# Dispatch sums in two parts, in two PSUM banks, around the second head's maxima

## The chip, the cores and the metric

The kernel runs on one core of a Trainium2 chip. The metric is the device time of one execution in microseconds (us), as a median of several executions. Times inside an execution come from one profiled execution, counted from the start of its span.

## The reference

Causal attention over 8 batches of 12 heads (448 tokens, 64 wide) gives `x`, 3584 tokens by 768. A soft mixture of experts follows, with 8 experts of 4 slots each, 32 slots in all:

```python
logits = x @ phi                              # 3584 x 32
d = exp(logits - logits.max(0)); d /= d.sum(0) + 1e-09    # over the tokens
slot_input = d.T @ x                          # 32 x 768: the dispatch
h = maximum(slot_input[e] @ w1[e], 0); slot_out[e] = h @ w2[e]
c = exp(logits - logits.max(1)); c /= c.sum(1) + 1e-09    # over the slots
out = c @ slot_out
```

All inputs are float32.

## The kernel before

**Stages.** Attention runs over 48 pairs of heads, six pairs to a batch. `block(p)` works on pair `p` (heads `a = 2p` and `a + 1`) while it prepares heads `a + 2` and `a + 3`; 47 blocks (p = 0 to 46) and a shorter last one take the first three quarters of the time. The experts and the output follow, with the expert weights streaming in. No scheduler moves anything: every engine runs its instructions in the order in which the code is written, and the framework adds the waits between engines from the tiles that the instructions read and write.

**A block on TensorE.** `scores2(a)` finishes the scores of head `a` by adding its row maxima (the four matmuls `s<-r,k`); `scores1_all(a + 2)` starts the scores of head `a + 2`, and its first matmul puts the mask into the second bank of its tile (`s<-tri,identb`); then the same two steps for heads `a + 1` and `a + 3`. `attv_pair` multiplies the weights of both heads by the values (`po<-va,pt`). At the end of the block come the small pieces for the experts, then the transpose of the second head's maxima (`max_row(a + 3, 0)`, shown as `s<-ident,r`) and four transposes of attention outputs (`xm<-ident,x`). The next block begins again with `scores2`.

**Three score tiles.** `s_[0]` to `s_[2]` are PSUM tiles of 128 x 1024 float32, two banks of 512 columns each, used in turn. At the end of block `p` the tile `m = s_[(a + 1) % 3]` is free, and it serves as scratch: the pieces for the experts are written to it, and the transposed maxima to its last 128 columns. In the next block `scores1_all` fills the same tile with the scores of a new head.

**The way of the maxima.** VectorE finds the maxima of head `a + 3` (`max_keys`), TensorE transposes them into `m`, VectorE reduces them to one row (`max_row(a + 3, 1)`, shown as `mr<-s`), GpSimd spreads that row (`r<-mr`), and the next block's second `scores2` reads it.

**The pieces for the experts.** A batch's slot logits are summed over its six pairs in `lt` (`logits_t`). Its dispatch `d.T @ x` is computed in the blocks of the following batch: `dispatch_a` multiplies on TensorE (`s<-x,gs`, in four column groups, one for each 128 tokens; a float32 matmul stands as two records in the profile), and `dispatch_b` is one VectorE instruction, `si = al * si + m` (`SCALAR_TENSOR_TENSOR si<-si,al,s`), which adds the product to the running sum. What a block does depends on `p % 6`:

- `p % 6 = 3` (p = 9 to 45, seven blocks): two matmul groups for the logits, 128 columns of dispatch, then `mr`, `lt`, `si`. Block 3 has the logits alone.
- `p % 6 = 4` (p = 10 to 40, six blocks): 256 columns of dispatch in the second bank, then `mr`, `si`.
- `p % 6 = 0` (p = 12 to 42, six blocks): 384 columns of dispatch in the first bank, then `mr`, `si`.
- `p % 6 = 1` and `5` have logits alone, `2` has neither.

VectorE goes on with `norm(p, 2)` (`x<-po,sm`) at the head of the next block.

Of the kernel before, what the change touches and what calls it, by code (L numbers as in the profile page):

```python
# [17 lines left out]
P = 128  # L18
# [64 lines left out]
def attention_soft_moe(ctx: ExitStack, tc: tile.TileContext, qk, va, phi, w, out):  # L83
# [52 lines left out]
    def loads_v(p, eng=nc.sync):  # L136
        if p < NPAIR:
            eng.dma_start(out=va_[p % 2], in_=va[p])
# [30 lines left out]
    def load_w(n):  # L169
        if n < len(order):  # L170
            t = wtiles[order[n]] = slot(n, f"w{n}")
            q, g, c = place(n), (n + 2) // 4, WN * ((n + 2) % 4)
            if n < RES or n == NBUF or q >= RES + LATE2:
                nc.sync.dma_start(out=t, in_=w[g, :, c:c + WN])
            elif 4 <= q < RES and n > NBUF:
                if q % 4 == 3:
                    nc.sync.dma_start(out=group(n), in_=w[g])
            elif n % 2:
                t = group(n)
                nc.sync.dma_start(out=t[:, 2 * WN:] if q < RES else t, in_=w[g, :, c - WN:c + WN])  # L180
# [39 lines left out]
    def misc(name):  # L220
        return ps_1.tile([P, 512], F32, tag="m", name=name)
# [88 lines left out]
    def max_row(i, k, w=RW - RF, to=None):  # L310
        if i >= NHD:
            return
        if k == 0:
            st["rt", i] = misc(f"rt{i}") if to is None else to
            if w == AW:
                nc.tensor.matmul(st["rt", i][0:w, 0:P], r_[i % 2][:, RF:RF + w], ident, start=True, stop=True)
            else:
                nc.tensor.transpose(out=st["rt", i][0:w, 0:P], in_=r_[i % 2][:, RF:RF + w], identity=ident)
        else:
            mr = st["mr", i] = wk.tile([NQB, 32], F32, tag="mr", name=f"mr{i}", bufs=2)  # L320
            nc.vector.tensor_reduce(out=mr, in_=st.pop(("rt", i))[0:NQB, 0:P].rearrange("p (g t)->p t g", g=4),
                                    axis=AX.X, op=ALU.max, negate=True)
# [12 lines left out]
    def scores2(i, cs):  # L335
        if i >= NHD:
            return
        p, h = divmod(i, 2)
        s = st["s", i]
        k2 = k2_  # L340
        for c in cs:
            o, w, m = KS * h + P * c, S - CQ0[c], min(P, KS - P * c)
            nc.tensor.matmul(s[0:m, SCOL[c]:SCOL[c] + w], k2[:, o:o + m],
                             r2[:, h, CQ0[c]:S], start=False, stop=True, skip_group_check=True)
# [60 lines left out]
    def norm(p, k):  # L405
        if k == 0:
            sm = st["sm", p] = moe.tile([P, NQ], F32, tag="sm", name=f"sm{p}", bufs=2)
            nc.vector.tensor_scalar(out=sm, in0=po2[:, :, HD], scalar1=EPS, scalar2=None, op0=ALU.add)
        elif k == 1:
            nc.vector.reciprocal(out=st["sm", p], in_=st["sm", p])  # L410
        else:
            x, sm = x_of(p), st.pop(("sm", p))
            m = NCH - 1
            nc.vector.tensor_tensor(out=x[:, 0:m].rearrange("p c (h d)->p h c d", h=2),
                                    in0=po2[:, 0:2 * m, 0:HD].rearrange("p (h c) d->p h c d", h=2),
                                    in1=sm[:, 0:2 * m].rearrange("p (h c)->p h c", h=2).unsqueeze(3)
                                    .to_broadcast([P, 2, m, HD]), op=ALU.mult)
            for h in range(2):
                a = AW * h
                nc.vector.tensor_scalar(out=x[0:AW, m, HD * h:HD * h + HD], in0=po2[a:a + AW, 2 * m, 0:HD],  # L420
                                        scalar1=sm[a:a + AW, 2 * m:2 * m + 1], scalar2=None, op0=ALU.mult)
# [22 lines left out]
    def logits_t(j, g):  # L444

        nc.vector.tensor_tensor(out=lt, in0=g, in1=lt if j else mk, op=ALU.add)
# [31 lines left out]
    def dispatch_a(b, hf, sp, sl=slice(0, 384)):  # L478
        dn = st["dn", b]
        x, n = st["xn", 2 * b + hf], sl.stop - sl.start  # L480
        for c in range(NCH):

            nc.tensor.matmul(sp[32 * c:32 * c + 32, 0:n], dn[:, c], x[:, c, sl],
                             start=True, stop=True, skip_group_check=True)

    def dispatch_b(b, hf, sp, sl=slice(0, 384)):
        s = si[:, 384 * hf + sl.start:384 * hf + sl.stop]
        nc.vector.scalar_tensor_tensor(out=s, in0=s, scalar=st["al", b][:, 0:1], in1=sp[:, 0:sl.stop - sl.start],
                                       op0=ALU.mult, op1=ALU.add)
# [74 lines left out]
    def block(p):  # L564
        a, b = 2 * p, p // 6 - 1
        m6 = p % 6
        if p + 1 < NPAIR:
            loads_v(p + 1, nc.sync if p + 1 < NPAIR - 1 else nc.scalar)
        if p % 2 and p < 44 or p in (16, 30):
            load_w(st["w"])  # L570
            st["w"] += 1

        if p:
            norm(p - 1, 2)
        scores2(a, range(NCH))
        exps(a)
        if p == 0:
            copy_k2(0, h1)
            cast_q(1, h1)
            warm(START[3], pob)  # L580
            max_row(1, 0)
            max_row(1, 1)
            max_spread(1)
            sub_k(1, h1, nc.vector)
        elif p > 1:
            xcopy(p - 2)
            if p == NPAIR - 2:
                sub_q(p + 1, h0)
        scores1_all(a + 2)
        if p == 0:  # L590
            warm(START[2], pob)
        for k in range(3):
            max_keys(a + 2, k)
        if p == 0:
            cast_k(2, h0)
        scores2(a + 1, range(NCH))
        exps(a + 1)
        if p == 0:
            cast_k(2, h1)
        scores1_all(a + 3)  # L600
        if m6 == 2 and p > 6:
            logits_b(b)
        max_keys(a + 3, 0)
        late_k = p == 1
        if p == 1:
            sub_q(2, h0)
            sub_k(3, h0)
            sub_q(2, h1)
            load_qk(4, 0)
        elif p:  # L610
            sub_k(p + 2, h0 if late_k else slice(0, 2))
            if not late_k:
                load_qk(p + 4, 1)
            sub_q(p + 1, h1 if p == NPAIR - 2 else slice(0, 2))
            load_qk(p + 3, 0)
        else:
            sub_q(1, h0)
            sub_q(1, h1)
            load_qk(3, 0)
            sub_k(2, h0)  # L620
        copy_k2(p + 1)
        if m6 == 2 and p > 6:
            logits_d(b, lt)
        if p:
            cast_k(p + 3)
            cast_q(p + 2)
        else:
            cast_q(2)
            cast_k(3)
        if m6 == 3 and p > 6:  # L630
            logits_al(b)
        elif m6 == 4 and p > 6:
            logits_n(b)
        attv_pair(p)
        max_row(a + 2, 1)
        max_spread(a + 2)
        if p == 0:
            sub_k(2, h1)
            load_qk(4, 1)
        for k in (1, 2):  # L640
            max_keys(a + 3, k)
        for k in range(2):
            norm(p, k)

        m = s_[(a + 1) % 3]
        parts = []
        if m6 in (1, 3, 5) and p > 1:
            j = (m6 + 3) % 6
            logits_a(b if m6 == 1 else p // 6, (j, j + 1), m[:, 0:P])
        elif m6 == 2 and p > 6:  # L650
            logits_e(b, m, 0)
        if m6 == 3 and p > 6:
            parts = [(b, 0, slice(0, P), 512)]
        elif m6 == 4 and p > 6 and p < NPAIR - 2:
            parts = [(b, 0, slice(P, 3 * P), 512)]
        elif m6 == 0 and p > 6:
            parts = [(b - 1, 1, slice(0, 3 * P), 0)]
        for d, hf, sl, o in parts:
            dispatch_a(d, hf, m[:, o:o + sl.stop - sl.start], sl)
        max_row(a + 3, 0, to=m[:, 1024 - P:1024])  # L660
        max_row(a + 3, 1)
        if m6 == 2 and p > 6:
            logits_e(b, m, 1)
        max_spread(a + 3)
        if late_k:
            sub_k(p + 2, h1)
            load_qk(p + 4, 1)
        if m6 in (1, 3, 5) and p > 1:
            logits_t(j, m[:, 0:P])
        for d, hf, sl, o in parts:  # L670
            dispatch_b(d, hf, m[:, o:o + sl.stop - sl.start], sl)
        if p:
            xtrans(p - 1)

    for p in range(NPAIR - 1):
        block(p)
# [5 lines left out]
    i, b, p = NHD - 1, NB - 1, NPAIR - 1  # L682
# [70 lines left out]
    parts = [(hf, slice(a, a + 192)) for hf in range(2) for a in (0, 192)]  # L753
# [255 lines left out]
```

## Time and profile before

| | |
|---|---|
| median of 3 runs | 396.43 us (396.28 to 396.48) |
| the profiled execution | 396.08 us, of which the span of its instructions is 394.4 us |
| blocks and last block | to about 300 us |
| TensorE matmuls busy | 366.3 us, 93% of the span |
| VectorE, ScalarE, GpSimd busy | 295.2, 282.9 and 256.5 us |
| DMA | 119.17 MB, 302 GB/s over the span |

PE is TensorE's matmuls, PEld its weight loads, DVE VectorE, ACT ScalarE, POOL GpSimd. In a row of the timeline stand the start in us, the duration in us (of all instructions of a merged row together), the engine, the code line, the operation with the tile written, an arrow and the tiles read, the shapes and the count; in brackets the idle time of the engine before it, and what ended that. Nearly every row names line 67, the helper through which each instruction passes, so rows are told apart by their tiles.

### The profile page before, as it was taken

The numbers are of one execution on the slowest core, as the hardware profiler recorded it, in microseconds if no ns is written. First come the engines' busy times: TensorE is split into PE (matmuls) and PEld (weight loads), VectorE is DVE, ScalarE is ACT, GpSimd is POOL, SyncE is SP. The second block draws the span as 40 slices with busy tenths as digits, with TensorE's granted clock in tenths as the row PEclk, the third lists the DMA queues.
The fourth block names the chain that finished last, engine by engine and source line by source line (L and its number), as shares of the span: only waits on it lengthen the run. The fifth ranks groups of instructions, "written<-read, shape, count | busy, mean of one in ns | idle before, by whom it ended". The sixth has DMA issues, their size and how long they took to land.

```text
span 394.4 us, 13997 instructions
## 1 busy us (share of the span) xinstructions
PE 366.3 (93%) x5763; PEld 293.9 (75%) x5763; DVE 295.2 (75%) x835; ACT 282.9 (72%) x397; POOL 256.5 (65%) x215
## 2 busy tenths in 40 slices
PE   7899999999999999999999999999999989988940
PEld 3689889888988998898889888988986544533420
DVE  7887889888888888898888988888886675342550
ACT  5888899898898898888988988888864012431440
POOL 5998899898898888898988988889860000000000
PEclk9999999999999999999999999999999999998985
DMA  7868877788898788777997877887579999999996
GB/s 250 277 229 281 288 288 237 251 273 274 274 318 272 244 270 300 257 246 248 307 323 256 286 240 249 275 287 250 183 246 399 422 431 428 429 421 419 433 429 295
DMA packets 28720, 119.17 MB, mean 302 GB/s; under 512 B 3440, under 2 KB 3952, under 8 KB 26480
## 3 DMA queue, kind: packets, MB, share of 16 engines
q1 hardware_dynamic: 28512, 118.01, 83.2%
q8 instruction: 45, 0.74, 0.7%
q10 hardware_dynamic: 144, 0.27, 0.2%
q14 instruction: 19, 0.16, 0.1%
HBM read 107.25 MB, written 11.01 MB: 300 GB/s over the span
## 4 chain that ended last, share of the span: by engine, by line
PE 67%; DMA 9%; POOL 9%; DVE 5%; ACT 4%; issue 2%; SPq 0%; POOLq 0%; DVEq 0%; ACTq 0%
PE s L67 34%; PE po L67 20%; DMA w<-in_w_dram 8%; POOL r L67 6%; PE xm L67 4%; POOL ks L67 3%; PE so L67 2%; PE e L67 2%; PE pp L67 2%; PE rt L67 2%; DMA kraw<-in_qk_dram 1%; ACT qd L67 1%; DVE lm L67 1%; DVE lg L67 1%; ACT w L67 1%
## 5 line engine op out<-in xcount | busy, mean ns | idle before, releaser
L67 DVE TRANSPOSE_TENSOR_REDUCE r<-s 128x32 f32<-128x1024 f32 x96 | 119.5, 1245 | 7.7 <-PE s L67 4.9
L67 ACT ACTIVATE pt<-s 128x1024 f32<-128x1024 f32 x96 | 98.8, 1029 | 31.0 <-PE s L67 24.0
L67 PEld LDWEIGHTS po<-va,pt 128*64 128x64 f32 x3008 | 102.3, 138 | 11.8 <-issue 11.3
L67 PE MATMUL po<-va,pt 128*64 128x65 f32 x3008 | 109.2, 224 | 0.0
L67 POOL TENSOR_TENSOR r<-qraw,qd 64x896 fp32r<-64x896 f32 (+1 forms) x50 | 99.4, 1989 | 1.9 <-ACT qd L67 1.8
L67 POOL TENSOR_TENSOR ks<-kraw,ks 64x896 fp32r<-64x896 f32 (+1 forms) x48 | 89.7, 1870 | 4.1 <-ACT ks L67 0.5
L67 POOL TENSOR_SCALAR_AFFINE_SELECT r<-mr 14x448 fp32r<-14x448 f32 x96 | 61.6, 643 | 32.9 <-DVE mr L67 28.6
L67 PE MATMUL s<-qd,ks 128*66 128x64 f32 (+3 forms) x384 | 80.6, 321 | 0.0
L67 PE MATMUL s<-r,k 128*128 128x448 f32 (+3 forms) x384 | 65.2, 291 | 2.7 <-POOL r L67 2.7
L67 PEld LDWEIGHTS s<-r,k 128*128 128x128 f32 (+1 forms) x384 | 59.3, 176 | 8.6 <-POOL r L67 5.9
L67 PEld LDWEIGHTS s<-qd,ks 128*128 128x128 f32 (+1 forms) x384 | 52.5, 183 | 2.1 <-issue 0.9
L67 ACT ACTIVATE ks<-kraw 128x896 fp32r<-128x896 f32 (+1 forms) x49 | 45.0, 920 | 5.6 <-DMA kraw<-in_qk_dram 4.4
L67 ACT ACTIVATE k<-ks 64x896 fp32r<-64x896 f32 (+1 forms) x49 | 45.8, 936 | 1.2
L67 ACT ACTIVATE qd<-qraw 128x896 fp32r<-128x896 f32 (+1 forms) x48 | 44.6, 929 | 0.9 <-POOL r L67 0.7
L67 PE MATMUL s<-tri,identb 128*128 128x192 bf16 x192 | 39.6, 270 | 0.6
L67 DVE TENSOR_REDUCE r<-r 128x16 f32<-128x32 f32 x192 | 33.7, 176 | 5.0
L67 DVE TENSOR_REDUCE mr<-s 14x32 f32<-14x128 f32 x47 | 13.1, 279 | 21.4 <-ACT qd L67 14.8
L67 PE MATMUL xm<-ident,x 128*128 128x128 f32 x188 | 28.3, 273 | 0.0
L67 ACT ACTIVATE xts<-xm 128x512 f32<-128x512 f32 x46 | 27.2, 591 | 0.4 <-PE xm L67 0.4
L67 DVE TENSOR_SCALAR x<-po,sm 64x64 f32<-64x64 f32 x94 | 25.9, 276 | 0.7
L67 DVE COPY w<-pp 128x384 f32<-128x384 f32 x28 | 14.5, 553 | 15.4 <-PE pp L67 15.3
L67 DVE TENSOR_TENSOR x<-po,sm 128x384 f32<-128x384 f32 x47 | 25.2, 537 | 0.0
(151 smaller groups left out, 397.9 us busy)
## 6 DMA issues: line engine op xcount, KB each, us to landing
w<-in_w_dram SPq DMA_DIRECT2D x34, 768.0 KB, 6.7
kraw<-in_qk_dram SPq DMA_DIRECT2D x46, 448.0 KB, 4.4
qraw<-in_qk_dram SPq DMA_DIRECT2D x46, 448.0 KB, 4.5
w<-in_w_dram SPq DMA_DIRECT2D x5, 3072.0 KB, 25.0
va<-in_va_dram SPq DMA_DIRECT2D x47, 260.0 KB, 4.8
out_dram<-w SPq DMA_DIRECT2D x7, 1536.0 KB, 12.6
w<-in_w_dram SPq DMA_DIRECT2D x5, 1536.0 KB, 11.2
qk<-in_qk_dram SPq DMA_DIRECT2D x2, 448.0 KB, 7.1
```

Of the source, the lines that this page charges most:

```text
L67: return self._tc.keep_in_program_order(op(*args, **kwargs))
```

## The change

The two large dispatches are cut in two. The first part goes to the first bank of `m`, and its sum stands directly behind its matmuls in the code, ahead of the second part's matmuls and of the maxima; the second part goes to the second bank and its sum stays where the sum was. Where `p % 6 = 4` the parts are 128 and 128 columns wide, where `p % 6 = 0` they are 192 and 192. Where `p % 6 = 3` the dispatch stays whole, and the addition of the logits moves ahead of the maxima.

```diff
         elif m6 == 4 and p > 6 and p < NPAIR - 2:
-            parts = [(b, 0, slice(P, 3 * P), 512)]
+            parts = [(b, 0, slice(P, 2 * P), 0), (b, 0, slice(2 * P, 3 * P), 512)]
         elif m6 == 0 and p > 6:
-            parts = [(b - 1, 1, slice(0, 3 * P), 0)]
+            parts = [(b - 1, 1, slice(0, 192), 0), (b - 1, 1, slice(192, 384), 512)]
         for d, hf, sl, o in parts:
             dispatch_a(d, hf, m[:, o:o + sl.stop - sl.start], sl)
+            if o == 0:
+                dispatch_b(d, hf, m[:, 0:sl.stop - sl.start], sl)
+        if m6 == 3 and p > 1:
+            logits_t(j, m[:, 0:P])
         max_row(a + 3, 0, to=m[:, 1024 - P:1024])
         max_row(a + 3, 1)
...
-        if m6 in (1, 3, 5) and p > 1:
+        if m6 in (1, 5) and p > 1:
             logits_t(j, m[:, 0:P])
         for d, hf, sl, o in parts:
-            dispatch_b(d, hf, m[:, o:o + sl.stop - sl.start], sl)
+            if o:
+                dispatch_b(d, hf, m[:, o:o + sl.stop - sl.start], sl)
```

What stands on TensorE at the end of block 12 (`p % 6 = 0`), before; `s_80` is `m`, `r_91` the maxima of head `a + 3`, and the word in brackets names the semaphores that an instruction waits for:

```order
L67 MATMUL s_80<-x_97,gs 32x384 x4
L67 MATMUL s_80<-ident,r_91 76x128 [waits DVE_49]
L67 MATMUL xm_1463<-ident,x_99 128x128 [waits PE_49]
L67 MATMUL xm_1463<-ident,x_99 128x128 x3
L67 MATMUL s_81<-r_93,k_92 128x448 [waits Activation_49,Pool_49]
L67 MATMUL s_81<-r_93,k_92 128x320
L67 MATMUL s_81<-r_93,k_92 128x192
L67 MATMUL s_81<-r_93,k_92 66x64
L67 LDWEIGHTS identb
L67 MATMUL s_80<-tri_117,identb 128x192 [waits DVE_49]
```

and now:

```order
L67 MATMUL s_80<-x_97,gs 32x192 x4
L67 MATMUL s_80<-x_97,gs 32x192 [waits DVE_49]
L67 MATMUL s_80<-x_97,gs 32x192 x3
L67 MATMUL s_80<-ident,r_91 76x128
L67 MATMUL xm_1473<-ident,x_99 128x128 [waits PE_49]
L67 MATMUL xm_1473<-ident,x_99 128x128 x3
```

The wait for VectorE has moved from the transpose to the first matmul of the second part, ahead of it in TensorE's queue.

VectorE at the same place, before (`po` is what `attv_pair` wrote):

```order
L67 TENSOR_SCALAR sm_1451<-po 128x7 [waits PE_49]
L67 RECIPROCAL sm_1451<-sm_1451 128x7 [waits DVE_49]
L67 TENSOR_REDUCE mr_1459<-s_80 14x32 [waits PE_49,Activation_49,Pool_49]
L67 SCALAR_TENSOR_TENSOR si<-si,al_1109,s_80 128x384
L67 TENSOR_TENSOR x_97<-po,sm_1451 128x2x3x64 [waits DVE_49]
```

and now:

```order
L67 TENSOR_SCALAR sm_1456<-po 128x7 [waits PE_49]
L67 RECIPROCAL sm_1456<-sm_1456 128x7 [waits DVE_49]
L67 SCALAR_TENSOR_TENSOR si<-si,al_1109,s_80 128x192 [waits PE_49,Activation_49]
L67 TENSOR_REDUCE mr_1469<-s_80 14x32 [waits PE_49,Pool_49]
L67 SCALAR_TENSOR_TENSOR si<-si,al_1109,s_80 128x192
L67 TENSOR_TENSOR x_97<-po,sm_1456 128x2x3x64 [waits DVE_49]
```

The first sum stands ahead of `mr` with a wait of its own for TensorE, and the second is half as wide as the sum was.

VectorE at the end of block 9 (`p % 6 = 3`), before:

```order
L67 RECIPROCAL sm_1150<-sm_1150 128x7 [waits DVE_49]
L67 TENSOR_REDUCE mr_1166<-s_80 14x32 [waits PE_49,Activation_49,Pool_49]
L67 TENSOR_TENSOR lt<-s_80,mk 128x128
L67 SCALAR_TENSOR_TENSOR si<-si,al_1109,s_80 128x128 [waits Activation_49]
L67 TENSOR_TENSOR x_99<-po,sm_1150 128x2x3x64 [waits DVE_49]
```

and now:

```order
L67 RECIPROCAL sm_1150<-sm_1150 128x7 [waits DVE_49]
L67 TENSOR_TENSOR lt<-s_80,mk 128x128 [waits PE_49,Activation_49]
L67 TENSOR_REDUCE mr_1167<-s_80 14x32 [waits PE_49,Pool_49]
L67 SCALAR_TENSOR_TENSOR si<-si,al_1109,s_80 128x128 [waits Activation_49]
L67 TENSOR_TENSOR x_99<-po,sm_1150 128x2x3x64 [waits DVE_49]
```

The addition to `lt` has changed places with `mr` and now waits for TensorE itself. TensorE's own rows there read the same as before, with the transpose waiting for VectorE; in the code the addition to `lt` now stands ahead of that transpose.

## The prediction

> **What bounds the kernel now.** I read the page's busy times, then the stages, then the timeline of TensorE and VectorE in single blocks, then the instructions on `si`.
>
> ```profile
> PE 366.3 (93%) x5763; PEld 293.9 (75%) x5763; DVE 295.2 (75%) x835; ACT 282.9 (72%) x397; POOL 256.5 (65%) x215
> 16.50:290.00 273.50, 271.06 (x4626) 240.39 (x4625) 232.36 (x653) 240.44 (x304) 240.41 (x186) 1.00 0.79 263
> 306.00:394.40 88.40, 66.39 (x751) 33.74 (x740) 39.16 (x114) 22.72 (x58) 0.00 (x0) 0.91 0.97 412
> ```
>
> The second and third rows are stages: length, then busy time of PE, PEld, DVE, ACT and POOL, granted clock, DMA share, GB/s. In the blocks PE is busy for 271.06 of 273.50 us, DMA at 0.79: TensorE's queue is the bound, and a hold there lengthens the block unless a later hold shrinks. After the blocks DMA is at 0.97, with transfers that follow the blocks; nothing there can make up for a later start.
>
> A block without dispatch is the measure, here the end of block 13 and the head of block 14:
>
> ```profile
> 94.82 0.30 PE L67 MATMUL s<-ident,r 128*76 128x128 f32 x1
> 95.87 0.26 PE L67 MATMUL s<-tri,identb 128*128 128x192 bf16 x1
> 96.07 1.03 ACT L67 ACTIVATE pt<-s 128x1024 f32<-128x1024 f32 x1 [0.89 <-PE s L67]
> 97.15 0.24 PE L67 MATMUL s<-tri,identb 128*128 128x192 bf16 x1
> ```
>
> From the transpose of the maxima to the first mask matmul are 1.05 us. The second mask matmul comes 0.05 us after the end of the exponentials (96.07 + 1.03 = 97.10), whose tile it overwrites, so it stands at transpose + 2.33 at the earliest. Now block 12 (`p % 6 = 0`):
>
> ```profile
> 87.89 0.85 PE L67 MATMUL s<-x,gs 128*32 128x384 f32 x8
> 88.68 0.30 PE L67 MATMUL s<-ident,r 128*76 128x128 f32 x1
> 89.97 0.24 PE L67 MATMUL s<-tri,identb 128*128 128x192 bf16 x1
> 91.14 0.26 PE L67 MATMUL s<-tri,identb 128*128 128x192 bf16 x1
> 88.20 0.20 DVE L67 RECIPROCAL sm<-sm 128x7 f32<-128x7 f32 x1
> 89.12 0.28 DVE L67 TENSOR_REDUCE mr<-s 14x32 f32<-14x128 f32 x1 [0.72 <-ACT qd L67]
> 89.33 0.59 DVE L67 SCALAR_TENSOR_TENSOR si<-si,al,s 128x384 f32<-128x384 f32 x1
> ```
>
> The first mask matmul comes 1.29 us after the transpose, 0.05 after the end of the sum (89.92): a hold of 0.24. This hold is what the change can take away. But it shows more: the sum reads columns 0 to 383, the first bank, and that matmul writes columns from 512 on, the second; the maxima, which did stand in the second bank, were read by 89.40. So the wait goes by the whole tile, not by the bank. Of the 0.24, only 0.13 reaches the block's length: the second mask matmul is at transpose + 2.46, and 2.33 is the exponentials' floor.
>
> **The change, part by part.** In the new order the first sum stands between the two parts' matmuls. The first matmul of the second part waits for VectorE, though of VectorE's work it reads only `x` and `gs`, finished blocks ago; it can only be waiting for the sum that reads its tile. So a chain that TensorE did not have lies ahead of the transpose: first part, its sum, second part. The pieces:
>
> - Hand-over from TensorE to VectorE: block 12's transpose ends at 88.98, `mr` starts at 89.12, 0.14. The shortest in the trace is 0.04, in block 10 from the last value matmul (76.04) to `sm`:
>
> ```profile
> 75.70 0.34 PE L67 MATMUL po<-va,pt 128*64 128x65 f32 x3
> 76.08 0.17 DVE L67 TENSOR_SCALAR sm<-po 128x7 f32<-128x7 f32 x1
> ```
>
>  I take 0.14, since the new sums wait for PE and Activation as `mr` did, and keep 0.04 for the range.
> - Hand-over back: 0.05, sum to mask matmul, above.
> - Widths: 8 matmul records take 0.85 us at 384 columns and 0.64 at 256 (below), 0.21 per 128: 0.53 at 192, 0.43 at 128. The row of 128 columns below has 0.40, without a start of its own. The transpose starts 0.06 to 0.07 before the last one ends.
> - Sums: 0.33 us at 128 columns (block 9, below), 0.40 at 192, from the four at the end of attention:
>
> ```profile
> L67 DVE SCALAR_TENSOR_TENSOR si<-si,al,e 128x192 f32<-128x192 f32 x4 | 1.4, 398 | 0.1
> L67 DVE SCALAR_TENSOR_TENSOR si<-si,al,s 128x384 f32<-128x384 f32 x6 | 3.6, 592 | 0.0
> ```
>
> *`p % 6 = 0`, six blocks.* First part 87.89 + 0.53 = 88.42; hand-over 88.56 (the reciprocal is done at 88.40); sum to 88.96; second part 89.01 to 89.54; transpose 89.48 instead of 88.68, +0.80. `mr` follows 0.44 later, the second sum 0.21 after that, at 90.13, to 90.53; the mask matmul can go at 90.58, where TensorE arrives at 89.48 + 1.05 = 90.53. The old hold is nearly gone, but the second mask matmul is at 89.48 + 2.33 = 91.81, against 91.14: **+0.67 each, 4.0 in all**.
>
> *`p % 6 = 4`, six blocks*, by block 10:
>
> ```profile
> 75.97 0.64 PE L67 MATMUL s<-x,gs 128*32 128x256 f32 x8
> 76.54 0.30 PE L67 MATMUL s<-ident,r 128*76 128x128 f32 x1
> 77.70 0.24 PE L67 MATMUL s<-tri,identb 128*128 128x192 bf16 x1
> 78.87 0.26 PE L67 MATMUL s<-tri,identb 128*128 128x192 bf16 x1
> 76.28 0.20 DVE L67 RECIPROCAL sm<-sm 128x7 f32<-128x7 f32 x1
> 77.19 0.46 DVE L67 SCALAR_TENSOR_TENSOR si<-si,al,s 128x256 f32<-128x256 f32 x1
> ```
>
> First part to 76.40, sum 76.54 to 76.87 (behind the reciprocal, 76.48), second part 76.92 to 77.35, transpose 77.28 instead of 76.54. Second mask matmul 77.28 + 2.33 = 79.61, against 78.87: **+0.74 each, 4.4 in all**. Here the hold was 0.11 and gave nothing to win.
>
> *`p % 6 = 3`, seven blocks*, by block 9:
>
> ```profile
> 70.14 0.40 PE L67 MATMUL s<-x,gs 128*32 128x128 f32 x8
> 70.47 0.30 PE L67 MATMUL s<-ident,r 128*76 128x128 f32 x1
> 72.88 0.26 PE L67 MATMUL s<-tri,identb 128*128 128x192 bf16 x1
> 71.13 0.27 DVE L67 TENSOR_TENSOR lt<-s,mk 128x128 f32<-128x128 f32 x1
> 71.33 0.33 DVE L67 SCALAR_TENSOR_TENSOR si<-si,al,s 128x128 f32<-128x128 f32 x1
> ```
>
> The addition to `lt` now precedes the transpose in the code, and reads the tile that the transpose writes. It can start 0.14 after the last matmul written there (70.54), at 70.68, and ends at 70.95; transpose 71.00 instead of 70.47. Second mask matmul 73.33 against 72.88: **+0.45 each, 3.2 in all**. Block 3 has the same move without a dispatch and without an old hold: its logits end 0.07 after the transpose's start, as elsewhere, so 0.07 + 0.14 + 0.27 + 0.05: **+0.53**.
>
> *Beside the path.* Twelve more sums make VectorE busier by about 12 x 0.2 = 2.4 us; they lie in its idle time ahead of `mr` (0.72 in block 12) and are charged above only where TensorE waits for them. `x<-po,sm` behind them comes earlier relative to TensorE. GpSimd gets the maxima later; its cover:
>
> ```profile
> 89.47 0.64 POOL L67 TENSOR_SCALAR_AFFINE_SELECT r<-mr 14x448 fp32r<-14x448 f32 x1 [0.71 <-DVE mr L67]
> 94.27 0.64 POOL L67 TENSOR_SCALAR_AFFINE_SELECT r<-mr 14x448 fp32r<-14x448 f32 x1
> 95.32 0.72 PE L67 MATMUL s<-r,k 128*128 128x448 f32 x4
> ```
>
> From one of these selects GpSimd works without a pause to the next, which ends at 94.91; TensorE needs it at 95.32, 0.41 spare. Block 12's maxima come 0.80 later, TensorE 0.67, so 0.28 is left and it costs nothing. No DMA is added or moved, and SP's and POOL's queues stay as they were.
>
> Sum: 4.0 + 4.4 + 3.2 + 0.5 = 12.1 us. Against the profiled execution's 396.08 that is 408.2; the median of the runs is 0.35 above that execution, 408.5. I forecast **408.4 us**.
>
> **A rule that speaks for the change.** The Trainium skill, "PSUM — Partial Sum Buffer", section "Summary: rules for kernel authors", advises that whoever reads PSUM while a matmul runs should have the matmul in a different bank; by that rule the first sum and the second part's matmuls could overlap. The trace does not bear it out for this program: block 12's mask matmul waits out a sum in the other bank. The time by the rule is the first rival's.
>
> **The rivals.**
>
> 1. *Waits by bank: faster.* If the first sum and the second part ran together, the transposes would stay where they are, the holds would go, and only the exponentials' floor would be left: 0.13 in six blocks, 0.08 in seven (72.88 against 70.47 + 2.33), nothing where `p % 6 = 4`. That is 1.3 us, 394.8 by the profiled execution, 395.1 by the median. It decides from the point where the wait on the second part is over before that part's turn. For it: VectorE idles there anyway. Against it: the wait stands there for nothing else, and block 12's wait across banks.
> 2. *Only the split parts hold.* If the transpose where `p % 6 = 3` waits for its maxima alone, as its unchanged row would allow, 3.7 us fall away: 404.7. Against it: one tile, and `lt` ahead in the code.
> 3. *A lower granted clock.* Pauses of some 0.6 us in 19 blocks could cost clock: it is 1.00 in the blocks and 0.91 in the last stage, where PE is busy for 66.39 of 88.40 us. At 0.98 the blocks would take 273.5 x 0.02 = 5.5 us more, 414. Against it: PE would stay busy for 95% of the blocks.
>
> **How the numbers follow.** Forecast 0.86, rival 1 0.04, rival 2 0.05, rival 3 0.04, no measurable change by something unseen 0.01. Unknown costs: hand-overs of 0.04 in 20 places would take 2.0 away, and the hold before the second mask matmul coming back only by half another 1; second parts as slow to start as 0.64 for 128 columns are the far end at +2.5, of which I take 2. Range 405.0 to 410.5, which leaves out the three rivals. This kernel's runs tell 0.2% from no change: faster 0.04, same 0.01, slower 0.95.
>
> **What would show it.** Right: from the first dispatch matmul to the transpose 1.59 us where `p % 6 = 0` (0.79 now) and 1.31 where 4 (0.57 now); the dispatch as two rows with the first sum between them; TensorE's idle time ahead of the second part and of the transpose put down to `si` and `lt`; the first mask matmul about 1.05 to 1.10 after the transpose everywhere. Wrong: transposes at their old distances (rivals 1 and 2), a granted clock below 1.00 in the blocks (rival 3), or `s<-r,k` waiting for POOL.

## The result and the profile after

The changed kernel takes 407.31 us (median, 406.92 to 407.45); the kernel before took 396.36 us beside it. The ratio is 1.0277, 95% interval 1.0262 to 1.0293: slower by 11 us, where 408.4 us had been forecast. The profiled execution after is 407.45 us with a span of 405.7 us. First the page's busy times, then the two stages of the prediction (length, then busy time of PE, PEld, DVE, ACT and POOL, granted clock, DMA share, GB/s):

```profile
PE 367.9 (91%) x5859; PEld 294.6 (73%) x5859; DVE 298.5 (74%) x847; ACT 282.5 (70%) x397; POOL 256.7 (63%) x215
16.89:301.52 284.63, 272.05 (x4723) 240.93 (x4722) 235.79 (x665) 239.81 (x304) 240.46 (x186) 1.00 0.77 253
317.30:405.70 88.40, 66.62 (x751) 33.78 (x746) 39.37 (x115) 22.81 (x58) 0.00 (x0) 0.91 0.98 413
```

The last row is drawn with the length that the stage had before, 88.40 us, and TensorE, VectorE and ScalarE are busy in it for as long as before to within 0.3 us. Told by one instruction, the start of its first expert matmuls (`e<-w,slt`), the last stage lies 11.53 us later and the span ends 11.3 us later, so it is 0.2 us shorter. The blocks are 11.13 us longer (284.63 against 273.50), and TensorE is busy there for only 0.99 us more. So TensorE stands still for some 10 us more. The view of waits says for whom (us in total, times, longest):

```profile
PE s L67 <- DVE si L67: 6.9, 12, 0.6
PE s L67 <- DVE lt L67: 3.9, 8, 0.5
...
PE s L67 <- POOL r L67: 2.7, 7, 0.9
```

The first two rows do not stand among the waits of before; 12 and 8 are the number of split dispatches and of moved additions to `lt`. The third row is the same in both. Block 12 (`p % 6 = 0`) on TensorE and VectorE:

```profile
89.96 0.53 PE L67 MATMUL s<-x,gs 128*32 128x192 f32 x8
91.10 0.53 PE L67 MATMUL s<-x,gs 128*32 128x192 f32 x8 [0.60 <-DVE si L67]
91.56 0.30 PE L67 MATMUL s<-ident,r 128*76 128x128 f32 x1
92.63 0.25 PE L67 MATMUL s<-tri,identb 128*128 128x192 bf16 x1
93.89 0.24 PE L67 MATMUL s<-tri,identb 128*128 128x192 bf16 x1
90.63 0.41 DVE L67 SCALAR_TENSOR_TENSOR si<-si,al,s 128x192 f32<-128x192 f32 x1 [0.16 <-PE s L67]
92.18 0.39 DVE L67 SCALAR_TENSOR_TENSOR si<-si,al,s 128x192 f32<-128x192 f32 x1
```

The first part ends at 90.49, its sum starts 0.14 later and takes 0.41, the second part starts 0.06 after that, though it goes to another bank and reads nothing that VectorE is writing. The transpose is 1.60 us behind the first dispatch matmul, where it was 0.79. The old hold is nearly gone: the first mask matmul comes 1.07 after the transpose, was 1.29; the second comes at 2.33, the floor that the exponentials set. Block 10 (`p % 6 = 4`) and block 9 (`p % 6 = 3`):

```profile
77.37 0.42 PE L67 MATMUL s<-x,gs 128*32 128x128 f32 x8
78.33 0.42 PE L67 MATMUL s<-x,gs 128*32 128x128 f32 x8 [0.54 <-DVE si L67]
78.69 0.30 PE L67 MATMUL s<-ident,r 128*76 128x128 f32 x1
77.93 0.35 DVE L67 SCALAR_TENSOR_TENSOR si<-si,al,s 128x128 f32<-128x128 f32 x1
71.14 0.40 PE L67 MATMUL s<-x,gs 128*32 128x128 f32 x8
72.02 0.30 PE L67 MATMUL s<-ident,r 128*76 128x128 f32 x1 [0.48 <-DVE lt L67]
71.68 0.29 DVE L67 TENSOR_TENSOR lt<-s,mk 128x128 f32<-128x128 f32 x1 [0.49 <-PE s L67]
```

In block 10 the transpose is 1.32 behind the first dispatch matmul (0.57 before); in block 9 it waits out the addition to `lt`.

One thing became shorter that the prediction had not seen. In the middle of the value matmuls stands the transpose of the other head's maxima (`rt`). In block 13, behind block 12's dispatch, first before, then after:

```profile
91.95 0.92 PE L67 MATMUL po<-va,pt 128*64 128x65 f32 x24
92.75 0.29 PE L67 MATMUL rt<-ident,r 128*64 128x128 f32 x1
```

```profile
94.68 0.92 PE L67 MATMUL po<-va,pt 128*64 128x65 f32 x24
95.43 0.27 PE L67 MATMUL rt<-ident,r 128*64 128x128 f32 x1
```

It came 0.80 us after the first value matmul and now comes 0.75 after it, as in the blocks without a dispatch. VectorE had been behind by the late sum, and its maxima with it: a third hold, of 0.03 to 0.05 us, that cost the row of value matmuls 0.06 to 0.07 in each of 19 blocks.

### The profile page after: what moved, and what is told of

Its sections match the earlier page's. It is cut to its first block, busy times and chain, and to the rows that moved or that the text cites. A ratio compares the mean times of both kernels' runs of the same rounds, so it can differ in the third digit from the quotient of the medians.

```text
span 405.7 us, 14221 instructions
## 1 busy us (share of the span) xinstructions
PE 367.9 (91%) x5859; PEld 294.6 (73%) x5859; DVE 298.5 (74%) x847; ACT 282.5 (70%) x397; POOL 256.7 (63%) x215
## 4 chain that ended last, share of the span: by engine, by line
PE 73%; DMA 10%; POOL 6%; DVE 5%; issue 2%; ACT 1%; DVEq 0%; POOLq 0%; SPq 0%
PE s L67 37%; PE po L67 22%; DMA w<-in_w_dram 10%; PE xm L67 5%; POOL r L67 4%; PE e L67 2%; PE so L67 2%; PE pp L67 2%; POOL ks L67 2%; PE rt L67 1%; DVE si L67 1%; PE warm L67 1%; ACT w L67 1%; DVE lt L67 1%; DVE sm L67 1%
## 5 line engine op out<-in xcount | busy, mean ns | idle before, releaser
L67 PEld LDWEIGHTS po<-va,pt 128*64 128x64 f32 x3008 | 101.5, 138 | 11.8 <-issue 11.3
L67 PE MATMUL po<-va,pt 128*64 128x65 f32 x3008 | 108.0, 223 | 0.0
```

The lines of the kernel that those rows point to most:

```text
L67: return self._tc.keep_in_program_order(op(*args, **kwargs))
```

## The experiments

Each but the one with wider first parts is an edit of the kernel before. Where dispatches stand ahead of the values, the first column is without them. The table has, from each trace, medians over the blocks from 7 on, in ns, for `p % 6` = 3 / 4 / 0: from the start of the last value matmul to the transpose of the maxima; from there to the first of the keys' matmuls (`s<-r,k`), between which `xm` stands; and from the last of those to the first mask matmul (some 33 is no wait).

| kernel | ratio, 95% interval | to the transpose | to the keys' matmuls | to the mask |
|---|---|---|---|---|
| before | 1 | 945 / 720 / 934 | 497 / 497 / 496 | 207 / 145 / 277 |
| after | 1.0277 (1.0262 to 1.0293) | 1498 / 1472 / 1752 | 496 / 497 / 497 | 33 / 32 / 47 |
| `lt` moved alone | 1.0085 (1.0072 to 1.0098) | 1497 / 721 / 934 | 496 / 496 / 496 | 35 / 144 / 278 |
| split alone, sum early | 1.0222 (1.0206 to 1.0238) | 944 / 1472 / 1752 | 498 / 497 / 498 | 208 / 33 / 47 |
| split alone, both sums late | 1.0034 (1.0022 to 1.0047) | 944 / 726 / 939 | 498 / 496 / 496 | 208 / 271 / 402 |
| split, first part in another tile | 1.0024 (1.0015 to 1.0033) | 944 / 726 / 939 | 497 / 732 / 695 | 207 / 33 / 35 |
| after, wider first parts | 1.0323 (1.0305 to 1.0342) | 1499 / 1540 / 1887 | 496 / 497 / 498 | 34 / 32 / 32 |
| dispatch ahead of the values | 1.0124 (1.0105 to 1.0142) | 726 / 151 / 152 | 1294 / 514 / 647 | 34 / 33 / 34 |
| `xm` later | 1.0134 (1.0119 to 1.0148) | 944 / 721 / 934 | `xm` behind them | |
| the same, dispatch in its own tile | 1.0150 (1.0136 to 1.0164) | 944 / 721 / 934 | `xm` behind them | |
| small first parts, 3 and 0 | 1.0113 (1.0096 to 1.0130) | 944 / 721 / 939 | 1369 / 496 / 522 | 34 / 142 / 117 |
| small first part, 0 alone | 0.9996 (0.9986 to 1.0006) | 944 / 721 / 939 | 497 / 497 / 525 | 208 / 144 / 118 |
| 3 and 0, `al` sooner | 0.9987 (0.9977 to 0.9996) | 944 / 721 / 939 | 586 / 496 / 522 | 34 / 144 / 118 |

### The two halves of the change, each alone

```diff
+        if m6 == 3 and p > 1:
+            logits_t(j, m[:, 0:P])
         max_row(a + 3, 0, to=m[:, 1024 - P:1024])
...
-        if m6 in (1, 3, 5) and p > 1:
+        if m6 in (1, 5) and p > 1:
```

> The kernel before with one edit: in blocks with p%6 = 3 the logits' transpose lt is issued ahead of the first head's maxima, the dispatch stays whole. Theory (the chain through VectorE, whose unit is the whole tile): only these seven blocks and block 3 change. There the transpose of the maxima waits for dispatch, lt and maxima in a row, 945 to about 1500 ns after the last attention matmul, and the hold of the first mask matmul and of rt behind lt is gone; net 0.41 us in each of seven and 0.55 in block 3, 3.4 us in all: 399.8 us, ratio 1.009. Rival (a wait by bank, the maxima on bank 0 free of the dispatch in bank 1): the transpose stays near 945 ns and only the hold goes, 0.1 to 0.2 us in each of seven: about 395, ratio 0.997.

Measured: 399.01 us against 395.78, ratio 1.0085. The transposes of the seven blocks moved from 945 to 1497 ns, the hold of the mask and that of `rt` went in six of them (block 45 is told below), block 3 moved by 0.55 us. The banks are not as the expectation has them: `lt` reads the first bank and the transposed maxima go to the second, so a wait by bank would have left the transposes where they were. So the transpose waits for the addition that reads its tile, and the rival that only the split parts hold is out.

The split alone (only the lines for `p % 6 = 0` and the early sum are shown; the sum behind the maxima is then the second part's):

```diff
-            parts = [(b - 1, 1, slice(0, 3 * P), 0)]
+            parts = [(b - 1, 1, slice(0, 192), 0), (b - 1, 1, slice(192, 384), 512)]
...
             dispatch_a(d, hf, m[:, o:o + sl.stop - sl.start], sl)
+            if o == 0:
+                dispatch_b(d, hf, m[:, 0:sl.stop - sl.start], sl)
```

> The kernel before with the other edit alone: the dispatches of blocks with p%6 = 0 and 4 in two parts in two banks, the first part's sum ahead of the maxima, the second's behind; lt where it was. Theory (chain first part, sum, second part): transposes 934 to about 1750 ns and 720 to about 1470 ns, net 0.60 us and 0.67 us in six blocks each, 7.6 us in all: 404.0 us, ratio 1.019; with the gain or loss of the move of lt alone it adds up to the changed kernel's 11 us. Rival (a wait by bank): transposes within 0.25 us of before, 396 us or below.

Measured: 404.58 us, ratio 1.0222, which is 8.8 us where 7.6 were expected. The distances are those of the changed kernel, and 12 blocks at their medians give 7.7 us. In this trace two of these blocks, 16 and 30, lose 0.35 and 0.30 us beyond that, and block 23, which has no dispatch, loses 0.21. Block 16, TensorE and VectorE:

```profile
113.43 0.43 PE L67 MATMUL s<-x,gs 128*32 128x128 f32 x8
114.75 0.43 PE L67 MATMUL s<-x,gs 128*32 128x128 f32 x8 [0.89 <-DVE si L67]
114.35 0.35 DVE L67 SCALAR_TENSOR_TENSOR si<-si,al,s 128x128 f32<-128x128 f32 x1 [0.41 <-PE s L67]
```

The sum starts 0.49 us after the first part's end instead of 0.14, and no wait in the profile explains it. In blocks 23 and 30 it is not a sum: `mr` starts some 0.35 us late, in block 30 here:

```profile
204.11 0.28 DVE L67 TENSOR_REDUCE mr<-s 14x32 f32<-14x128 f32 x1 [1.28 <-PE xm L67]
```

With the move of `lt` alone block 16 loses 0.19 us (there the sum behind `mr` is late, and the mask waits 345 ns instead of 144) and block 45 loses 0.24 (its `mr` is late). What these places have in common is their number in VectorE's order: counted in the traces, with the waits that stand as instructions of their own, all five are the 320th, 448th, 576th or 832nd, so they lie 128 or a multiple of it apart. Three other runs, told below, have the 320th late too, and the traces show no VectorE instruction of the blocks late in this way at another place, though not each one at such a place is late. Where such a place falls on an instruction that TensorE does not wait for, as in the kernel before and in the changed one, nothing is lost. What VectorE does there was not tried.

So the two halves add up to 12.0 us, the whole change to 11.0. In the traces the blocks lose 3.8 and 8.6 us by the halves and 11.1 by the whole, and the 1.3 between them are what these five places cost.

### Is it the split, or the wait?

Both sums behind the maxima (the split lines alone, without the early call):

> The two parts in two banks, but both sums behind the maxima, as the one sum was before; lt where it was. Theory: nothing of VectorE stands between the two parts, so the transpose moves by the second part's extra matmul groups alone, 0.1 to 0.25 us; the two sums are longer than one by a fixed cost, so the first mask matmul waits about 0.15 us more: 0.3 to 0.4 us in each of twelve blocks, about 4 us: 400.5 us, ratio 1.010. Rival (it is the splitting and the extra VectorE instructions that cost, wherever the sum stands): as much as with the early sum, 7 to 8 us, 404 us.

Measured: 397.0 us, ratio 1.0034, 1.2 us instead of 4. The transposes moved by 5 ns, not by 100 to 250:

```profile
87.80 0.86 PE L67 MATMUL s<-x,gs 128*32 128x192 f32 x16
90.01 0.24 PE L67 MATMUL s<-tri,identb 128*128 128x192 bf16 x1 [0.21 <-DVE si L67]
```

The 16 records of 192 columns take 0.86 us; the 8 of 384 took 0.85. What is left is the longer work of two sums, 0.125 us more of the old hold in each of twelve blocks, 1.5 us. Splitting costs next to nothing on TensorE; my estimate for the extra matmul groups was wrong, and the 8.8 us are the early sum's.

Next the same instructions in the same order on TensorE and VectorE as with the early sum, and only the first part's tile changed (shown against the split alone):

```diff
-            dispatch_a(d, hf, m[:, o:o + sl.stop - sl.start], sl)
+            t = m if o else misc(f"d{p}")
+            dispatch_a(d, hf, t[:, o:o + sl.stop - sl.start], sl)
             if o == 0:
-                dispatch_b(d, hf, m[:, 0:sl.stop - sl.start], sl)
+                dispatch_b(d, hf, t[:, 0:sl.stop - sl.start], sl)
```

> The same instructions in the same order on TensorE and VectorE as with the early first sum (lt where it was), with one thing changed: the first part goes into a tile of its own in another PSUM slot, so that the second part has no sum of the same tile ahead of it. Theory (the second part waits for the sum because both lie in one tile): the wait of about 0.5 us goes, the transposes move by no more than 0.1 to 0.25 us for the extra matmul groups, and the shorter late sum takes the hold of the first mask matmul away: between 0 and 0.2 us in each of twelve blocks, about 0.9 us in all: 397.3 us, ratio 1.002. Rival (the splitting and VectorE's extra instructions cost, not the wait): about 7 us still, 403.5 us, ratio 1.018.

Measured: 396.71 us, ratio 1.0024; 0.9 us instead of 8.8. Block 12:

```profile
88.47 0.53 PE L67 MATMUL d<-x,gs 128*32 128x192 f32 x8
88.82 0.51 PE L67 MATMUL s<-x,gs 128*32 128x192 f32 x8
89.26 0.31 PE L67 MATMUL s<-ident,r 128*76 128x128 f32 x1
89.55 0.66 PE L67 MATMUL xm<-ident,x 128*128 128x128 f32 x4
89.96 0.72 PE L67 MATMUL s<-r,k 128*128 128x448 f32 x4
90.52 0.26 PE L67 MATMUL s<-tri,identb 128*128 128x192 bf16 x1
89.08 0.41 DVE L67 SCALAR_TENSOR_TENSOR si<-si,al,d 128x192 f32<-128x192 f32 x1
89.71 0.28 DVE L67 TENSOR_REDUCE mr<-s 14x32 f32<-14x128 f32 x1 [0.22 <-ACT qd L67]
```

The second part runs on from the first, while VectorE is still to sum; no wait, and the transpose is 0.79 behind the first dispatch matmul, as before the change. This decides it: the 0.60 us ahead of the second part was a wait for the sum of the same tile, not for a bank, the split or the place of the sum in VectorE's order. The bank rule of the Trainium skill ("PSUM — Partial Sum Buffer", "Summary: rules for kernel authors": whoever reads PSUM during a matmul does so from another bank) is not contradicted: with two tiles, VectorE's sum (89.08 to 89.49) does run beside the second part's matmuls (88.82 to 89.33). What the rule needs here besides is that the two banks are two tiles.

The total came out as expected, but not by the expected way. The extra groups cost 5 ns; instead the four `xm`, whose slot the first part had, now wait for its sum (89.49) and start at 89.55, and the keys' matmuls come 0.20 and 0.24 us later. That is 2.6 us in twelve blocks. Against it stand the holds that went.

### Does the sum's length set the chain?

The changed kernel with first parts of 192 and 320 columns (of 256 and 384):

```diff
-            parts = [(b, 0, slice(P, 2 * P), 0), (b, 0, slice(2 * P, 3 * P), 512)]
+            parts = [(b, 0, slice(P, P + 192), 0), (b, 0, slice(P + 192, 3 * P), 512)]
...
-            parts = [(b - 1, 1, slice(0, 192), 0), (b - 1, 1, slice(192, 384), 512)]
+            parts = [(b - 1, 1, slice(0, 320), 0), (b - 1, 1, slice(320, 384), 512)]
```

> The changed kernel with wider first parts: 320 and 64 columns instead of 192 and 192 where p%6 = 0, 192 and 64 instead of 128 and 128 where p%6 = 4. All the same instructions, the same matmul columns in all. Theory (TensorE waits out the first sum): only the first sum's length enters, 0.53 us at 320 columns (between 0.46 at 256 and 0.59 at 384) against 0.40 at 192, and 0.40 at 192 against 0.33 at 128: transposes 1752 to about 1880 ns and 1472 to about 1540 ns, 6 x 0.13 + 6 x 0.07 = 1.2 us more than the changed kernel: ratio to the kernel before about 1.031. Rival (a fixed cost for each split, a hand-over or a switch, and not the sum): as the changed kernel, ratio 1.028, transposes where they were.

Measured: 408.53 us, ratio 1.0323; the transposes at 1540 and 1887 ns. Block 12 on TensorE and the groups of VectorE's sums with 320 columns:

```profile
89.96 0.75 PE L67 MATMUL s<-x,gs 128*32 128x320 f32 x8
91.44 0.32 PE L67 MATMUL s<-x,gs 128*32 128x64 f32 x8 [0.74 <-DVE si L67]
91.69 0.30 PE L67 MATMUL s<-ident,r 128*76 128x128 f32 x1
...
L67 DVE SCALAR_TENSOR_TENSOR si<-si,al,s 128x320 f32<-128x320 f32 x6 | 3.3, 547 | 2.2 <-PE s L67 2.2
```

TensorE's wait grows from 0.60 to 0.74 us, the sum from 0.40 to 0.55: it waits out the sum, and longer when the sum is wider. A fixed cost for each split would have left the transposes where they were.

### Can the hold be taken away without the chain?

Six versions tried that. First, the dispatch ahead of the block's value matmuls, in the slot that `rt` had, summed while VectorE waits for those matmuls:

```diff
+        for d, hf, sl in parts:
+            dt = misc(f"d{p}")
+            dispatch_a(d, hf, dt, sl)
+        attv_pair(p, m[:, 768:768 + P] if parts else None)
...
+        for d, hf, sl in parts:
+            dispatch_b(d, hf, dt, sl)
         for k in range(2):
             norm(p, k)
```

> A version meant to beat both. The kernel before, with each dispatch whole and issued ahead of the block's value matmuls into a PSUM slot of its own (the transposes of the first head's maxima, which had that slot, go to the free third part of the next head's tile); its one sum stands on VectorE between the block's key maxima and the normalisation, where VectorE waits for the value matmuls. Theory (the holds come from a sum that shares a tile with what TensorE writes next): the transposes stay at 945, 720 and 934 ns after the last value matmul less the dispatch's own time, which moves ahead; the holds of the first mask matmul (207, 145 and 277 ns) fall to some 35, those of the second come back at some 120, the 55 ns of rt go: 0.14 us in seven blocks, 0.07 in six, 0.21 in six, 2.7 us in all: 393.1 us, ratio 0.993. Rival: the early matmuls or the sum delay the value matmuls, the maxima or the transposes of x (whose slot the dispatch now has ahead of them, as with the first part in another tile, where that cost 0.2 us in each block): no gain, or up to 2.4 us slower, ratio 1.000 to 1.006.

Measured: 400.8 us, ratio 1.0124, a miss, and outside its rival's range too. The holds of the mask and of `rt` went, as expected. But where `p % 6 = 3` the keys' matmuls came 0.80 us later, since `xm` waited for VectorE, in seven blocks by the view of waits:

```profile
PE xm L67 <- DVE sm L67: 4.1, 7, 0.6
```

VectorE's sum ahead of it had waited for the factor `al` from ScalarE (9.6 us in these seven blocks); the run with small first parts (below) shows the same.

Then `xm` moved behind the first keys' matmuls, without and with the whole dispatch in a slot of its own:

```diff
         scores2(a, range(NCH))
+        if p > 1:
+            xtrans(p - 2)
         exps(a)
...
+        for d, hf, sl, o in parts:
+            t = misc(f"d{p}")
+            dispatch_a(d, hf, t, sl)
+            dispatch_b(d, hf, t, sl)
```

(The lower part is the second version's alone; the old calls go.)

> The kernel before with one edit: the four transposes of the attention output (xm) are issued behind the first keys' matmuls (s<-r,k) of the next block instead of ahead of them. Theory (a floor of the exponentials): the first exponentials wait for those keys' matmuls, which stood behind 0.6 us of xm; they now start up to 0.41 us sooner (the spare time of GpSimd's select), the second mask matmul's wait falls from 98 to 118 ns to some 34 in the 20 blocks with p%6 = 1, 2 and 5 and in the first ones, and the first mask matmul, which waits for the maxima, has xm as its cover as before: 1.4 to 2 us less, ratio 0.995 to 0.9965. Rival: the keys' matmuls wait for GpSimd's select instead, or xm behind them delays the masks: no gain, or slower by up to 0.2 us a block, ratio 1.00 to 1.02.

> Meant to beat both: xm behind the first keys' matmuls as in the run beside it, and each dispatch whole, in the PSUM slot that xm takes later, its one sum ahead of the first head's maxima on VectorE; where p%6 = 3 the dispatch stands ahead of the logits. Theory (a sum holds TensorE only through its tile, and with the dispatch in another tile and xm out of its way nothing of TensorE's waits for the sum): the transposes stay within 10 ns of 945, 720 and 934, the first mask matmul's wait falls from 207, 145 and 277 to 35 to 120 ns, rt loses its 50: 0.22 us in seven blocks, 0.16 in six, 0.21 in six, 3.8 us below the run beside it, and with that one's gain of 1.4 to 2: ratio 0.985 to 0.988. Rival: the sum of 384 columns (0.59 us) ahead of the maxima delays them, with them GpSimd's select, and the second keys' matmuls wait: the six blocks with p%6 = 0 give back 0.1 to 0.4 us each, ratio 0.989 to 0.995 with the other gains; or, if the wait is not of the tile but of the sum's place in the order, the transposes move by 0.5 us and more and it is slower than before.

Measured: 400.85 us, ratio 1.0134, and 401.47 us, 1.0150; both missed. The exponentials' floor did go (the second mask matmul no longer waits: 34 ns in all blocks). But the first version's waits have

```profile
PE s L67 <- POOL r L67: 6.1, 15, 1.1
```

where before had 2.7 in 7: without `xm` ahead of them the keys' matmuls wait for GpSimd, above all where `p % 6 = 2` (573 ns after the transpose, against 644 with `xm` ahead of them). Block 13 (`p % 6 = 1`), GpSimd's select and the keys' matmuls:

```profile
96.33 0.64 POOL L67 TENSOR_SCALAR_AFFINE_SELECT r<-mr 14x448 fp32r<-14x448 f32 x1
97.03 0.74 PE L67 MATMUL s<-r,k 128*128 128x448 f32 x4
```

The select ends at 96.97, and the matmuls come 145 ns after the transpose (496 before). Where it ends ahead of the transpose, as with `p % 6 = 0` and 3, they come after 60 ns. So in its old place `xm` takes 0.44 us of TensorE's queue, part of it time in which TensorE would wait for GpSimd anyway. At its new place it takes 0.47 (where `p % 6 = 1` the mask comes 499 ns behind the last of the keys' matmuls instead of 33) and covers nothing. The rival with GpSimd held, and with it goes the forecast of the second version. There the keys' matmuls wait less where `p % 6 = 2` (362 ns after the transpose), but longer where it is 1 and 4 (409 and 400 instead of 145 and 220): in block 12 the sum ahead of `mr` makes it start 0.66 us after the transpose instead of 0.45, and from the select that reads it GpSimd works without a pause to the one that block 13's keys need. The second version's own claim, that the transposes stay, stands nevertheless. In its block 12:

```profile
89.80 0.85 PE L67 MATMUL d<-x,gs 128*32 128x384 f32 x8
90.59 0.30 PE L67 MATMUL s<-ident,r 128*76 128x128 f32 x1
90.72 0.61 DVE L67 SCALAR_TENSOR_TENSOR si<-si,al,d 128x384 f32<-128x384 f32 x1 [0.41 <-PE d L67]
```

A sum of 384 columns stands ahead of the maxima in VectorE's order, and the transpose is where it was, 0.79 behind.

Last, small first parts of 128 columns in a slot of their own, `xm` in its old place:

```diff
+        if m6 in (0, 3) and p > 6:
+            e = (b, 0, misc(f"d{p}"), slice(0, P)) if m6 else (b - 1, 1, misc(f"d{p}"), slice(0, P))
+            dispatch_a(*e)
+            dispatch_b(*e)
...
-            parts = [(b - 1, 1, slice(0, 3 * P), 0)]
+            parts = [(b - 1, 1, slice(P, 3 * P), 0)]
```

> Meant to beat both, with xm left where it was. Where p%6 = 3 the whole dispatch (128 columns) goes to a PSUM slot of its own ahead of the logits and is summed at once, ahead of the maxima; where p%6 = 0 its first 128 columns do so, the other 256 stay in the maxima's tile and are summed behind the maxima; p%6 = 4 is as before. Theory (a sum holds TensorE only through its tile): transposes within 10 ns of 945 and 934; the small early sums end before xm needs the slot (in the first part of 192 columns it cost 0.2 us), so s<-r,k stays at 496; the first mask matmul's wait falls from 207 to 35 and from 277 to about 150, of which the exponentials' floor gives back 85 in the first kind and none in the second; rt loses 55 in the first and some in the second: 7 x 0.14 + 6 x 0.13 to 0.18 = 1.8 to 2.1 us, ratio 0.995. Rival 1 (the sum's place costs, whatever its tile): transposes 0.3 to 0.5 us later, 5 us slower, ratio 1.013. Rival 2 (xm still waits for the slot): s<-r,k later by 0.05 to 0.2 us in thirteen blocks, which takes the gain: ratio 0.998 to 1.002.

Measured: 400.56 us, ratio 1.0113. The ratio is near the first rival's, but not for its reason: the transposes stayed at 944 and 939 ns. Where `p % 6 = 0` it came nearly as expected. Where it is 3, ScalarE, VectorE and TensorE in block 9:

```profile
70.91 0.28 ACT L67 ACTIVATE al<-run_m,run_m 128x1 f32<-128x1 f32 x1
71.22 0.35 DVE L67 SCALAR_TENSOR_TENSOR si<-si,al,d 128x128 f32<-128x128 f32 x1 [0.84 <-ACT al L67]
71.63 0.66 PE L67 MATMUL xm<-ident,x 128*128 128x128 f32 x4 [0.65 <-DVE si L67]
```

The sum needs the factor `al`, which ScalarE computes only in these blocks and only behind its casts. It holds VectorE and, through the slot, `xm`. Neither the theory nor a rival had it. Two runs followed, the first without those seven blocks, the second with `logits_al` ahead of `cast_q`:

> Meant to beat both by little: only the part for p%6 = 0 of the run before (first 128 columns of the dispatch in a PSUM slot of its own, issued ahead of the logits' place and summed ahead of the maxima, the other 256 in the maxima's tile and summed behind); the other kinds as in the kernel before. Theory (a sum holds TensorE only through its tile): the six blocks as there, transposes +5 ns, s<-r,k +26, first mask matmul 277 to 117, second 34 to 60, rt -10: 0.11 us each, 0.7 us in all, ratio 0.998. Rival (the gain is given back elsewhere): ratio 1.000 or above.

> As the run with small early first parts where p%6 = 0 and 3, with one thing more: ScalarE computes al ahead of the cast of qd instead of behind it. Theory: where p%6 = 3 that run lost 0.87 us in each of seven blocks because the early sum needs al, which ScalarE had at 0.5 us after the transpose, and xm waits for the sum's slot; with al 0.9 us sooner the sum runs at once, xm and s<-r,k are on time, the first mask matmul's wait falls from 207 to 35, the second's comes back at 118, rt loses 55: 0.14 us less than before in seven blocks, with 0.11 in six: 1.7 us in all, ratio 0.996. Rival: qd, 0.28 us later, holds GpSimd's subtraction or the next masks, or xm waits all the same: ratio 1.000 to 1.01.

Measured: 395.8 us, ratio 0.9996, no difference to be measured, though the blocks of its trace are 0.66 us shorter, as expected; and 395.41 us, ratio 0.9987 (0.9977 to 0.9996), where 0.996 was expected. In the second, block 9 reads

```profile
70.07 0.28 ACT L67 ACTIVATE al<-run_m,run_m 128x1 f32<-128x1 f32 x1
70.45 0.35 DVE L67 SCALAR_TENSOR_TENSOR si<-si,al,d 128x128 f32<-128x128 f32 x1
70.85 0.66 PE L67 MATMUL xm<-ident,x 128*128 128x128 f32 x4
```

so the 0.87 us were `al`'s. Of the 1.7 us expected, the blocks of the trace have 0.88: `s<-r,k` still comes 0.09 late in seven blocks, and block 16 loses 0.19 to the 320th instruction of VectorE. This version is the fastest here, 0.6 us below the kernel before. The interval leaves out 1 by a little, but the median of the kernel before alone lies between 395.63 and 396.36 us from one measurement to another, so I do not count it as a gain; more of the holds was not won in any run.

## Why the prediction was right

- *The mechanism.* The wait by the whole tile, read from block 12's mask matmul, is what happened; the run with another tile shows it as the cause, and the run with wider parts shows its size. TensorE's new waits, 6.9 and 3.9 us, stand at the places named.
- *The chains.* `p % 6 = 0`: transposes +0.80 forecast, +0.82 measured; `p % 6 = 4`: +0.74 and +0.75; `p % 6 = 3` and block 3: +0.53 and +0.55. The hand-overs of 0.14 and 0.05 came out as 0.14 and 0.06; the low end of 0.04 for the first did not occur.
- *What comes back.* The holds of the first mask matmul went (-0.23, -0.11 and -0.17 where `p % 6` = 0, 4 and 3), and the second mask matmul, at the exponentials' floor, then waited 0.08 to 0.09 longer in each (by the working 0.11 where `p % 6` = 0 and 4).
- *The term that was mis-sized* is the net per block: in the same order +0.67, +0.74 and +0.45 forecast, +0.60, +0.67 and +0.40 measured from the last value matmul of a block to that of the next (block 3: +0.55 against +0.53). I counted two holds behind the late sum and there were three. The one of `rt`, further down, among the next block's value matmuls, gave back 0.06 to 0.07 in 19 blocks, 1.2 us; the chains, longer by 0.01 to 0.02 each, took 0.3 of it again. So the sum was 12.1 us and the blocks lost 11.1, which is the error of the forecast.
- *Beside the path.* GpSimd's cover held, its row of waits is unchanged. VectorE became busier by 3.3 us, not 2.4, and it cost nothing.
- *Luck.* The prediction has no term for VectorE's late instructions, and needed none, because in the changed kernel none of them fell where TensorE waits. With the split alone they cost 0.9 us of the 8.6.
- *The rivals.* Waits by bank: excluded by the 0.60 us. Only the split parts: excluded by the move of `lt` alone. A lower clock: the granted clock in the blocks is 1.00 in both.

## What to carry to other kernels

Before moving a reader of a shared scratch tile ahead of a writer, ask in what unit the waits are kept: here it is the tile, so two banks of one tile buy no overlap, and two tiles do, at the price of whoever owned the second slot. A hold that ends at another floor is worth less than it looks (0.24 us seen, 0.14 to win), and a late instruction can hold at several places, so follow it to the end of the next block. A piece brought forward takes all its operands with it: look for the one (`al`) that another engine makes just in time.

## What was not expected of the hardware

Two matmul groups of 192 columns in place of one of 384 cost 0.01 us (0.86 against 0.85), and the transpose behind them moved by 5 ns. Four `xm` took 0.44 us of TensorE's queue ahead of the keys' matmuls and 0.47 between these and the mask, but ahead of them part of that time would have been a wait for GpSimd. And in five kernels single instructions of VectorE started late with no wait to explain it: some 0.35 us late behind a wait, 0.18 where they follow another instruction directly. The eight that stand out all lie at places 128 or a multiple of it apart in VectorE's order. What happens there stays open.
